# A gated linear attention and a mixture of experts: the blanking DMA and the weight loads are queued elsewhere, and a range check moves to ScalarE

## The chip, the cores and the metric

The kernel runs on one core of a Trainium2 chip. The core has five engines with an instruction queue each: TensorE (PE; its weight loads are shown as PEld), VectorE (DVE), ScalarE (ACT), GpSimd (POOL) and SyncE (SP). An engine takes its instructions strictly in the order of its queue. Loads are issued from SP's queue; the blanking, the scatters and the output go out from POOL's. The metric is the device time of one execution in microseconds, the median of several runs.

## The reference

Two blocks. The first is a recurrence with a complex decay, for 4 batches, 8 heads, 768 steps and head size 48; the second sends each of the 3072 resulting rows of 384 numbers through one of eight experts (384 to 1024 to 384).

```python
mag = np.sqrt(a_re * a_re + a_im * a_im)
scale = np.minimum(mag, 0.999) / (mag + 1e-06)
a_re_n, a_im_n = (a_re * scale, a_im * scale)
for t in range(S):
    new_re = ar * S_re - ai * S_im
    new_im = ar * S_im + ai * S_re
    kv = np.einsum('bhd,bhe->bhde', k[:, :, t], v[:, :, t])
    S_re, S_im = (new_re + kv, new_im)
    y[:, :, t] = np.einsum('bhd,bhde->bhe', q[:, :, t], S_re)
...
logits = x @ w_gate
expert_idx = np.argmax(logits, axis=1)
...
    h = np.maximum(x_sorted[lo:hi] @ w1[e], 0.0)
    y_sorted[lo:hi] = h @ w2[e]
...
return (gate_w[:, None] * y).astype(np.float32)
```

## The kernel before

**Attention.** The rows are cut into 24 chunks of 128, and two chunks make a unit `u` (0 to 11). The decay of a unit is turned into logarithm and angle by five steps, `decay_steps`, that go back and forth between POOL (products of `ar` and `ai`), DVE and ACT (Ln and Exp, then Arctan in another table). `decay_sums` takes running sums of the logarithm on PE (`csl`) and turns them into two factors `E` and `Ei` on ACT; `decay_total` makes the factor `M` of a whole chunk from `ms`; `angle_sums` and `rotation` make cosine and sine, `CS`. For each chunk `attention` multiplies `q` and `k` by the factors (`product`: `Qe` and `Ke` on POOL, `Q` and `K` on DVE), transposes them (`tp`), forms scores `at`, masks them to `am`, and sums `y`, which ACT copies into `x`. While unit `u` is in its attention, the decay of unit `u + 1` is prepared. The copies `ar`, `ai`, `q`, `k`, `v` of a unit live in two buffers each, and `ai` is overwritten with the angle `th`, so that a load of `ai` waits until the angle sums of two units before are done.

**Routing.** Every four chunks, `route` picks an expert for 512 rows and scatters them into a DRAM buffer `xs` that has 448 places for each expert (`NS` = 3584 rows in all). Unused places must hold a zero row with an index that drops it, so `blank` writes 5.4 MB of `zrow` over `xs` ahead of the first scatter, from POOL's queue.

**Experts.** Each of eight experts reads its rows with `gather`, transposes them (`turn`), and computes in `expert` eight tiles `hps` of 128 hidden units by 448 rows (three matmuls each, in three PSUM buffers), which DVE (even ones) and ACT (odd ones) turn into `ht` in SBUF; then the products `yps` with `w2`, eight matmuls for each of four row tiles. The weights of expert 0 are loaded during the attention (`load_w(0)`, called at `u == 6`), the others two experts ahead.

**Range check.** The attention is only valid while `a_re` is not negative and the squared magnitude is at least 0.37. `range_check` reads both arrays again in 12 pieces of 128 by 768, three pieces for each of four experts, and `verdict` decides whether a slow path has to run; with this data it doesn't.

**What sets the order.** The program is written as above, but a scheduler decides in which order each engine's queue holds the instructions, by data, buffers, its own estimate of times, and by the pairs that `tc.add_manual_dep` ties together without a wait. So a tie moves neighbours too.

Of the kernel before, what the change touches and what calls it, by code (L numbers as in the profile page):

```python
# [35 lines left out]
def kernel(  # L36
# [12 lines left out]
    nc = tc.nc  # L49
# [6 lines left out]
    NT = N // P  # L56
# [25 lines left out]
    def const(shape, name, dt=FP):  # L82
        return cp.tile(shape, dt, name=name)
# [15 lines left out]
        out=last, in_=ones, compare_op=OP.is_ge, fill=0.0, base=1 - P, pattern=[[0, P]], channel_multiplier=1  # L99
# [19 lines left out]
    zrow = const([P, XW], "zrow")  # L119
# [5 lines left out]
    xs = dr.tile([ZR + P, XW], FP, name="xs")  # L125

    def blank():

        nc.gpsimd.dma_start(out=xs[0:NS].rearrange("(i p) c -> p i c", p=P), in_=bc(zrow, 1, NS // P))
        nc.gpsimd.dma_start(out=xs[ZR : ZR + P], in_=zrow)  # L130

    W_T = {}

    def load_w(e):
        a = wp[e % 2].tile([P, KD, F], FP, tag="w1", name="w1t")
        nc.sync.dma_start(out=a, in_=w1[e].rearrange("(i p) f -> p i f", p=P))
        b = wp[e % 2].tile([P, KF, DM], FP, tag="w2", name="w2t")
        T["w"] = nc.sync.dma_start(out=b, in_=w2[e].rearrange("(i p) d -> p i d", p=P))
        W_T[e] = a, b


    xl = ctx.enter_context(tc.tile_pool(name="xl", bufs=2))
    psL = ctx.enter_context(tc.tile_pool(name="psL", bufs=1, space=PSUM))
    att = ExitStack()
    ld = att.enter_context(tc.tile_pool(name="ld", bufs=2))
# [8 lines left out]
    T = {}  # L154

    def act(**kw):

        ins = nc.scalar.activation(**kw)  # L158
        if "act" in T:
            tc.add_manual_dep(ins.ins, T["act"].ins.name, NOSYNC, reason="table order")  # L160
        T["act"] = ins

    def table(name):
        ins = nc.scalar.preload_act_table_set(name)
        if "act" in T:
            tc.add_manual_dep(ins.ins, T["act"].ins.name, NOSYNC, reason="table order")
        T["act"] = ins

    def load(u, names):
        for nm, src in names:  # L170
            t = ld.tile([P, U, H, D], FP, tag=nm, name=nm)
            for c in range(U):
                b, s = divmod(u * U + c, CB)
                nc.sync.dma_start(out=t[:, c], in_=src[b, :, s * P : (s + 1) * P, :].rearrange("h t d -> t h d"))
            T[nm, u] = t.rearrange("p c h d -> p (c h d)")

    def load_a(u):
# [97 lines left out]
    def product(u, c, nm, src, dec):  # L275
        sl = slice(c * DM, (c + 1) * DM)
        e = ch.tile([P, H, D], FP, tag=nm + "e", name=nm + "e")
        nc.gpsimd.tensor_tensor(
            out=e.rearrange("p h d -> p (h d)"), in0=T[src, u][:, sl], in1=T[dec, u][:, sl], op=OP.mult
        )  # L280
        t = ch.tile([P, H, 2, D], FP, tag=nm, name=nm)
        nc.vector.tensor_tensor(out=t, in0=T["CS", u][:, c * H : (c + 1) * H], in1=bc(e, 2, 2), op=OP.mult)  # L282
        return t.rearrange("p h a d -> p h (a d)")
# [140 lines left out]
    for u in range(NU):  # L424
        if u + 1 < NU:
            load_qkv(u + 1)
        if u == 1:
            blank()
        steps = decay_steps(u + 1) if u + 1 < NU else []
        steps = steps[:2] + [lambda: decay_sums(u, 0)] + steps[2:4] + [lambda: decay_sums(u, 1)] + steps[4:]  # L430
        table("natural_log_exp_and_others")
        if u > GR // U and (u - 1) * U % GR == 0:
            route((u - 1) * U - GR, False)
        for f in steps:
            f()
# [92 lines left out]

    CW = 768
    NC = B * H * S * D // (P * CW)  # L530
    good = const([P, NC], "good")
    flat = [a.rearrange("b h s d -> (b h s d)").rearrange("(p n) -> p n", p=P) for a in (a_re, a_im)]

    def range_check(i):
        ar = ck.tile([P, CW], FP, tag="car", name="car")
        ai = ck.tile([P, CW], FP, tag="cai", name="cai")
        for t, a in zip((ar, ai), flat):
            ld = nc.sync.dma_start(out=t, in_=a[:, i * CW : (i + 1) * CW])
            tc.add_manual_dep(ld.ins, T["w"].ins.name, NOSYNC, reason="behind the weights")
        s = ck.tile([P, CW], FP, tag="cs", name="cs")  # L540
        nc.gpsimd.tensor_tensor(out=s, in0=ar, in1=ar, op=OP.mult)
        nc.gpsimd.tensor_tensor(out=ai, in0=ai, in1=ai, op=OP.mult)
        nc.gpsimd.tensor_tensor(out=s, in0=s, in1=ai, op=OP.add)
        nc.vector.scalar_tensor_tensor(out=s, in0=s, scalar=-MAG2_MIN, in1=ar, op0=OP.add, op1=OP.min)
        nc.vector.tensor_reduce(out=good[:, i : i + 1], in_=s, op=OP.min, axis=AX_X)

    def verdict():

        bad = xl.tile([P, NC], FP, tag="bad", name="bad")
        nc.vector.tensor_scalar(out=bad, in0=good, scalar1=0.0, scalar2=None, op0=OP.is_ge)  # L550
        nc.vector.tensor_scalar(out=bad, in0=bad, scalar1=-1.0, scalar2=1.0, op0=OP.mult, op1=OP.add)
        two = xl.tile([P, 2], FP, tag="two", name="two")
        nc.vector.reduce_sum(two[:, 0:1], bad, axis=AX_X)
        nc.vector.reduce_sum(two[:, 1:2], ov, axis=AX_X)
        nc.vector.tensor_tensor(out=two[:, 1:2], in0=two[:, 1:2], in1=two[:, 0:1], op=OP.add)
        bp = psX.tile([1, 2], FP, tag="tp", padded_shape=[1, 512], name="bp")
        mm(bp, ones[:, 0:1], two)
        nc.vector.tensor_copy(out=flag, in_=bp)

    flag = const([1, 2], "flag", I32)  # L560
    rest0 = [P] * ((CAP - FIRST) // P) + [HT]
    own = [P] * (CT - 1) + [HT]
    for e in range(E):
# [154 lines left out]
```

## Time and profile before

| what | value |
|---|---|
| median of 3 runs | 811.48 us (809.31 to 820.83) |
| profiled execution | 809.06 us, its span 807.4 us |
| mean granted TensorE clock | 0.89 |
| busy: PE, PEld | 698.9, 510.5 us |
| busy: DVE, POOL, ACT | 348.6, 278.1, 207.7 us |
| DMA | 79.60 MB, 99 GB/s over the span |

The profile is one execution. The span runs from the first to the last instruction; the execution's own time is 1.7 us longer. The attention fills about the first 465 us (the last copy of `y` starts at 464.9), the experts the rest. Times in a timeline are counted from the start of the span, and the bracket behind a row is the engine's idle time before it with what ended it.

### The profile page before, as it was taken

What the parts mean: (1) busy time and instruction counts of PE and PEld (TensorE: products, weight loads), DVE (VectorE), ACT (ScalarE), POOL (GpSimd) and SP (SyncE); (2) the same over time, 40 slices, a digit from 0 to 9 for tenths busy, and PEclk for the clock granted to TensorE, in tenths of its full rate; (3) what the DMA queues carried; (4) which work ended last, traced back from release to release, by engine and by line L of the source; (5) the groups of instructions that cost most, each with busy time, mean ns of one, the idle gap of its engine ahead of it and who ended that gap; (6) DMA issues with size and microseconds to landing.
All of it is one profiled execution on the core that took longest, in us unless ns stands there. A gap on an engine that the chain in (4) does not pass through costs nothing. (4 is left out here: it accounts for less than half of the span.)

```text
span 807.4 us, 9049 instructions
## 1 busy us (share of the span) xinstructions
PE 698.9 (87%) x3583; PEld 510.5 (63%) x3583; DVE 348.6 (43%) x577; ACT 207.7 (26%) x338; POOL 278.1 (34%) x216
## 2 busy tenths in 40 slices
PE   0057899989799998998989999999998989898994
PEld 0036788868689877887878977554544545454552
DVE  2137466655766767664555331202133342425211
ACT  3225343342526525344333110101010101000000
POOL 4353360643365255253321011000053443526101
PEclk9999879768878968885887889999999999999998
DMA  9952432233144243313010152523272635352000
GB/s 263 290 150 48 81 60 40 50 89 69 36 102 89 40 86 74 78 30 88 2 21 11 50 186 85 192 97 125 97 240 91 219 115 205 132 180 72 27 11 24
DMA packets 148817, 79.60 MB, mean 99 GB/s; under 512 B 127278, under 2 KB 139071, under 8 KB 148768
## 3 DMA queue, kind: packets, MB, share of 16 engines
q1 hardware_dynamic: 144032, 63.75, 29.7%
q0 software_dynamic: 4736, 15.20, 5.2%
q8 instruction: 30, 0.49, 0.2%
q14 instruction: 19, 0.16, 0.1%
HBM read 63.74 MB, written 15.98 MB: 99 GB/s over the span
## 5 line engine op out<-in xcount | busy, mean ns | idle before, releaser
L71 PE MATMUL hps<-xt,w1t 128*128 128x448 f32 (+2 forms) x432 | 154.9, 518 | 11.2 <-DVE ht L506 11.2
L71 PE MATMUL yps<-w2t,ht 128*128 128x384 f32 (+1 forms) x512 | 147.2, 488 | 0.0
L71 PEld LDWEIGHTS hps<-xt,w1t 128*128 128x128 f32 x432 | 83.0, 198 | 75.5 <-issue 58.6
L71 PEld LDWEIGHTS yps<-w2t,ht 128*128 128x128 f32 (+1 forms) x512 | 81.7, 177 | 64.7 <-issue 16.1
L487 POOL DMA_INDIRECT out_dram<-y,xg x32 | 31.1, 971 | 205.7 <-DVE y L515 174.0
L71 PE MATMUL y<-v,am 128*128 128x48 f32 x384 | 75.7, 292 | 0.0
L71 PE MATMUL y<-G,qt 96*128 96x48 f32 x320 | 69.0, 301 | 0.0
L71 PEld LDWEIGHTS y<-v,am 128*128 128x128 f32 x384 | 63.9, 213 | 4.3 <-DVE am L377 1.7
L515 DVE TENSOR_SCALAR y<-yps,xg 128x384 f32<-128x384 f32 x24 | 14.8, 617 | 113.8 <-PE yps L71 113.8
L71 PE MATMUL at<-qt,kt 96*128 96x128 f32 x384 | 59.3, 299 | 3.5 <-DVE am L377 3.2
L71 PE MATMUL csl<-LL,tri 128*128 128x384 f32 x48 | 25.5, 618 | 40.9 <-DVE LL L214 34.2
L71 PEld LDWEIGHTS at<-qt,kt 96*128 96x128 f32 x384 | 54.2, 211 | 9.1 <-issue 4.4
L71 PE MATMUL ms<-ones,LL 128*96 128x1 f32 x384 | 51.5, 267 | 8.0 <-ACT Ei L158 8.0
L71 PEld LDWEIGHTS ms<-ones,LL 128*96 128x96 f32 x384 | 51.5, 234 | 9.7 <-ACT Ei L158 9.1
L504 ACT ACTIVATE ht<-hps 128x448 f32<-128x448 f32 (+2 forms) x36 | 18.1, 503 | 150.5 <-PE hps L71 150.5
L71 PEld LDWEIGHTS y<-G,qt 96*128 96x128 f32 x320 | 56.0, 218 | 0.6 <-issue 0.6
L369 PE MATMUL tp<-ident,Q 128*96 128x128 f32 x192 | 40.4, 333 | 16.2 <-DVE Q L282 16.2
L349 POOL DMA_INDIRECT xs<-x,to x24 | 26.9, 1122 | 77.6 <-DMA xs<-x,to 34.4
L506 DVE TENSOR_SCALAR ht<-hps 128x448 f32<-128x448 f32 (+2 forms) x36 | 20.5, 570 | 74.6 <-PE hps L71 74.5
L258 DVE TENSOR_SCALAR r<-cst 128x384 f32<-128x384 f32 x24 | 13.4, 557 | 82.7 <-PE cst L71 82.7
L369 PE MATMUL tp<-ident,K 128*96 128x128 f32 x192 | 40.0, 328 | 5.3 <-DVE K L282 5.3
L200 POOL TENSOR_TENSOR A<-A,R 128x768 f32<-128x768 f32 x12 | 23.6, 1967 | 55.0 <-ACT R L158 44.4
(117 smaller groups left out, 1035.5 us busy)
## 6 DMA issues: line engine op xcount, KB each, us to landing
w1t<-in_moe_w_dram SPq DMA_DIRECT2D x8, 1536.0 KB, 6.3
w2t<-in_moe_w_dram SPq DMA_DIRECT2D x8, 1536.0 KB, 6.8
xs<-zrow POOLq DMA_DIRECT2D x1, 5404.0 KB, 20.0
ar<-in_a_re_dram SPq DMA_DIRECT2D x24, 192.0 KB, 3.2
ai<-in_a_im_dram SPq DMA_DIRECT2D x24, 192.0 KB, 3.4
q<-in_q_dram SPq DMA_DIRECT2D x24, 192.0 KB, 3.4
k<-in_k_dram SPq DMA_DIRECT2D x24, 192.0 KB, 3.6
v<-in_v_dram SPq DMA_DIRECT2D x24, 192.0 KB, 3.2
```

The source lines that it names most:

```text
L71: return nc.tensor.matmul(o, lhsT=lhsT, rhs=rhs, start=start, stop=stop, skip_group_check=True)
L200: nc.gpsimd.tensor_tensor(out=A, in0=A, in1=R, op=OP.mult)
L258: nc.vector.tensor_scalar(out=r, in0=cs, scalar1=MAGIC, scalar2=MAGIC, op0=OP.add, op1=OP.subtract)
L349: nc.gpsimd.indirect_dma_start(out=xs[:, :], out_offset=bass.IndirectOffsetOnAxis(ap=to[:, i : i + 1], axis=0), in_=x[:, i], in_offset=None,)
L369: nc.tensor.transpose(out=tp[0:DD, j], in_=X[:, hg * 4 + j], identity=ident)
L487: return nc.gpsimd.indirect_dma_start(out=out, out_offset=bass.IndirectOffsetOnAxis(ap=idx, axis=0), in_=y[0:m], in_offset=None, bounds_ch ...
L504: nc.scalar.activation(out=ht[:, f], in_=ps, func=AF.Relu)
L506: nc.vector.tensor_scalar(out=ht[:, f], in0=ps, scalar1=0.0, scalar2=None, op0=OP.max)
L515: nc.vector.tensor_scalar(out=y, in0=ps, scalar1=gate, scalar2=None, op0=OP.mult)
```

## The change

Three edits.

The blanking is called after the attention of chunk 0, and both of its DMAs are tied behind `T["K"]`, POOL's product `Ke` of that chunk. The first weight load of an expert, `w1`, is tied behind `T["ld"]`, the load that was written last when `load_w` is called; the second, `w2`, gets no tie. In the range check ACT makes both squares and finds violations with Relu and the running sum that an activation can write (`accum_out`); POOL keeps only the sum of the squares, and DVE does nothing until the verdict.

```diff
     def blank():
-        nc.gpsimd.dma_start(out=xs[0:NS].rearrange("(i p) c -> p i c", p=P), in_=bc(zrow, 1, NS // P))
-        nc.gpsimd.dma_start(out=xs[ZR : ZR + P], in_=zrow)
+        for o, i in ((xs[0:NS].rearrange("(i p) c -> p i c", p=P), bc(zrow, 1, NS // P)), (xs[ZR : ZR + P], zrow)):
+            queue(nc.gpsimd.dma_start(out=o, in_=i), T["K"])
...
+    def queue(ins, before):
+        tc.add_manual_dep(ins.ins, before.ins.name, NOSYNC, reason="queue order")
+        return ins
...
     def load_w(e):
         a = wp[e % 2].tile([P, KD, F], FP, tag="w1", name="w1t")
-        nc.sync.dma_start(out=a, in_=w1[e].rearrange("(i p) f -> p i f", p=P))
+        ins = nc.sync.dma_start(out=a, in_=w1[e].rearrange("(i p) f -> p i f", p=P))
+        queue(ins, T["ld"])
...
-                nc.sync.dma_start(out=t[:, c], in_=src[b, :, s * P : (s + 1) * P, :].rearrange("h t d -> t h d"))
+                T["ld"] = nc.sync.dma_start(out=t[:, c], in_=src[b, :, s * P : (s + 1) * P, :].rearrange("h t d -> t h d"))
...
-        nc.gpsimd.tensor_tensor(
+        T[nm] = nc.gpsimd.tensor_tensor(
...
-        if u == 1:
-            blank()
...
+        if u == 0:
+            blank()
...
         s = ck.tile([P, CW], FP, tag="cs", name="cs")
-        nc.gpsimd.tensor_tensor(out=s, in0=ar, in1=ar, op=OP.mult)
-        nc.gpsimd.tensor_tensor(out=ai, in0=ai, in1=ai, op=OP.mult)
+        nc.scalar.activation(out=s, in_=ar, func=AF.Square)
+        nc.scalar.activation(out=ai, in_=ai, func=AF.Square)
+        nc.scalar.activation(out=ar, in_=ar, func=AF.Relu, scale=-1.0, accum_out=bad[:, 0, i : i + 1])
         nc.gpsimd.tensor_tensor(out=s, in0=s, in1=ai, op=OP.add)
-        nc.vector.scalar_tensor_tensor(out=s, in0=s, scalar=-MAG2_MIN, in1=ar, op0=OP.add, op1=OP.min)
-        nc.vector.tensor_reduce(out=good[:, i : i + 1], in_=s, op=OP.min, axis=AX_X)
+        nc.scalar.activation(out=s, in_=s, func=AF.Relu, scale=-1.0, bias=mag2, accum_out=bad[:, 1, i : i + 1])
```

Lines of the kernel after are five higher in the attention. What the scheduler makes of it stands in three places.

POOL's queue at the start, before. In the names, `_137`, `_140` and `_160` belong to unit 0, `_153`, `_156` and `_189` to unit 1, `_338` and `_355` to unit 2; `Qe_255` and `Ke_259` are chunk 0.

```order
L129 DMA xs_106<-zrow_102 128x28x386
L200 TENSOR_TENSOR A_160<-A_160,R_162 128x768
L193 TENSOR_TENSOR A_189<-ar_153 128x768
L194 TENSOR_TENSOR R_191<-ai_156 128x768
L130 DMA xs_106<-zrow_102 128x386
L347 COPY x_325<-tidi_100 128x4
L213 TENSOR_TENSOR ai_140<-ai_140,A_160 128x768
L193 TENSOR_TENSOR A_355<-ar_338 128x768
L200 TENSOR_TENSOR A_189<-A_189,R_191 128x768
L278 TENSOR_TENSOR Qe_255<-q_143,E_201 128x384
L278 TENSOR_TENSOR Ke_259<-k_146,Ei_202 128x384
```

Here the blanking (L129) and the products of unit 1's load stand ahead of unit 0's `ai` product (L213), and a product of unit 2's load ahead of unit 1's L200. After, from unit 0's `ai` product on (`_340` and `_343` are unit 2 now, `Qe_422` is chunk 1):

```order
L218 TENSOR_TENSOR ai_140<-ai_140,A_160 128x768
L198 TENSOR_TENSOR A_189<-ar_153 128x768
L199 TENSOR_TENSOR R_191<-ai_156 128x768
L205 TENSOR_TENSOR A_189<-A_189,R_191 128x768
L283 TENSOR_TENSOR Qe_255<-q_143,E_201 128x384
L283 TENSOR_TENSOR Ke_259<-k_146,Ei_202 128x384
L130 DMA xs_106<-zrow_102 128x28x386
L218 TENSOR_TENSOR ai_156<-ai_156,A_189 128x768
L130 DMA xs_106<-zrow_102 128x386
L198 TENSOR_TENSOR A_355<-ar_340 128x768
L199 TENSOR_TENSOR R_357<-ai_343 128x768
L283 TENSOR_TENSOR Qe_422<-q_143,E_201 128x384
```

Unit 0's `ai` product moved ahead of unit 1's loads, unit 1's chain and chunk 0's products ahead of the blanking, and chunk 1's products behind the products of unit 2's loads.

SP's queue, before, from unit 1's last load on (`_338`, `_341`, `_344`, `_347` are unit 2, `ar_604` is unit 3; `w1t` and `w2t` are expert 0's weights).

```order
L174 DMA v_186<-in_v_dram 128x8x48 x2
L136 DMA w1t_1965<-in_moe_w1_dram 128x3x1024
L174 DMA ar_338<-in_a_re_dram 128x8x48 x2
L138 DMA w2t_1967<-in_moe_w2_dram 128x8x384
L174 DMA ar_604<-in_a_re_dram 128x8x48 x2
L174 DMA q_344<-in_q_dram 128x8x48 x2
L174 DMA k_347<-in_k_dram 128x8x48
L174 DMA ai_341<-in_a_im_dram 128x8x48 x2
```

After (`_340`, `_343`, `_346`, `_349` are unit 2, `ar_869` is unit 4):

```order
L179 DMA v_186<-in_v_dram 128x8x48 x2
L179 DMA ar_340<-in_a_re_dram 128x8x48 x2
L179 DMA ar_604<-in_a_re_dram 128x8x48 x2
L145 DMA w2t_1967<-in_moe_w2_dram 128x8x384
L179 DMA ai_343<-in_a_im_dram 128x8x48 x2
L179 DMA q_346<-in_q_dram 128x8x48 x2
L179 DMA k_349<-in_k_dram 128x8x48 x2
L179 DMA ar_869<-in_a_re_dram 128x8x48 x2
```

The load of `w1t` left this place for one behind unit 8's `ai`; `w2t` stayed, ahead of unit 2's `ai`, `q` and `k`.

ACT's queue beside a range check, before: transposed rows `xt`, the four odd hidden tiles, the last row tile's copy.

```order
L74 COPY xt_3960<-tp_3967 128x448
L504 ACTIVATE ht_3982<-hps_3988 128x448
L504 ACTIVATE ht_3982<-hps_3998 128x448
L504 ACTIVATE ht_3982<-hps_4008 128x448
L504 ACTIVATE ht_3982<-hps_4018 128x448
L522 COPY y_4066<-yps_4065 64x384
```

After, from behind the first odd hidden tile to ahead of the third (`car_3932`, `car_3942` and `car_3952` are the three pieces' `ar`, with `cai` and `cs` to match; `ht_3984<-hps_4000` is the second odd tile):

```order
L548 ACTIVATE cs_3936<-car_3932 128x768
L550 ACTIVATE car_3932,bad_3502<-car_3932 128x768
L549 ACTIVATE cai_3933<-cai_3933 128x768
L548 ACTIVATE cs_3946<-car_3942 128x768
L509 ACTIVATE ht_3984<-hps_4000 128x448
L552 ACTIVATE cs_3936,bad_3502<-cs_3936,mag2_3503 128x768
L549 ACTIVATE cai_3943<-cai_3943 128x768
L550 ACTIVATE car_3942,bad_3502<-car_3942 128x768
L548 ACTIVATE cs_3956<-car_3952 128x768
L552 ACTIVATE cs_3946,bad_3502<-cs_3946,mag2_3503 128x768
L550 ACTIVATE car_3952,bad_3502<-car_3952 128x768
L549 ACTIVATE cai_3953<-cai_3953 128x768
```

Eleven of the twelve new ACT instructions stand between the first and the third odd tile; the twelfth, `cs_3956` into `bad_3502`, stands between the third and the fourth.

## Rows read from the trace of the kernel before

**Rows 1.** windows: PE, PEld, DVE, ACT, POOL busy us (instructions), PEclk, DMA share, GB/s
```profile
0.00:20.00 20.00, 0.00 (x0) 0.00 (x0) 4.55 (x11) 6.78 (x7) 8.79 (x18) 1.00 0.95 262
...
120.00:160.00 40.00, 38.22 (x270) 34.25 (x269) 27.72 (x52) 16.09 (x26) 13.13 (x9) 0.84 0.24 47
```

**Rows 2.** timeline of POOL, start: start us, us, engine, line, op, tiles [idle before]
```profile
7.99 1.81 POOL L129 DMA_DIRECT2D xs<-zrow  x1
...
28.94 1.47 POOL L193 TENSOR_TENSOR A<-ar 128x768 f32<-128x768 f32 x1 [15.83 <-DMA ar<-in_a_re_dram]
...
33.21 2.52 POOL L213 TENSOR_TENSOR ai<-ai,A 128x768 f32<-128x768 f32 x1
43.53 1.47 POOL L193 TENSOR_TENSOR A<-ar 128x768 f32<-128x768 f32 x1 [7.80 <-DMA ar<-in_a_re_dram]
```

**Rows 3.** DMA queues and issues from 5 to 34 us: packets, MB; us to landing
```profile
q1 hardware_dynamic: 16405, 3.04, 56.2%
q0 software_dynamic: 1219, 5.55, 52.7%
...
xs<-zrow POOLq DMA_DIRECT2D x1, 5404.0 KB, 20.0
...
ar<-in_a_re_dram SPq DMA_DIRECT2D x2, 192.0 KB, 18.0
```

**Rows 4.** page, part 6: DMA issues of one line over the whole span
```profile
ar<-in_a_re_dram SPq DMA_DIRECT2D x24, 192.0 KB, 3.2
```

**Rows 5.** timeline of ACT, the first three units
```profile
14.13 1.72 ACT L158 ACTIVATE A<-A 128x768 f32<-128x768 f32 x2 [0.15 <-DVE A L201]
...
63.39 0.94 ACT L158 ACTIVATE CS<-fg,mhalfpi 128x768 f32<-128x768 f32 x1 [6.38 <-DVE fg L263]
...
65.81 1.28 ACT L164 ACT_TABLE_LOAD   x1
...
77.94 0.48 ACT L402 COPY x<-y 128x384 f32<-128x384 f32 x1 [3.00 <-PE y L71]
...
129.87 0.94 ACT L158 ACTIVATE CS<-fg,mhalfpi 128x768 f32<-128x768 f32 x1 [7.39 <-DVE fg L263]
...
170.00 0.94 ACT L158 ACTIVATE CS<-fg,mhalfpi 128x768 f32<-128x768 f32 x1 [2.21 <-DVE fg L263]
```

**Rows 6.** timeline of PE, the first two units' total-decay matmuls
```profile
50.21 5.28 PE L71 MATMUL ms<-ones,LL 128*96 128x1 f32 x32 [7.99 <-ACT Ei L158]
...
82.03 4.00 PE L71 MATMUL ms<-ones,LL 128*96 128x1 f32 x32
```

**Rows 7.** timeline of PE, experts 1 to 7
```profile
549.01 2.22 PE L478 MATMUL tp<-ident,xg 128*128 128x128 f32 x12
551.16 18.31 PE L71 MATMUL hps<-xt,w1t 128*128 128x448 f32 x48
569.31 18.37 PE L71 MATMUL yps<-w2t,ht 128*128 128x384 f32 x64
587.61 2.22 PE L478 MATMUL tp<-ident,xg 128*128 128x128 f32 x12
...
608.56 4.22 PE L71 MATMUL hps<-xt,w1t 128*128 128x448 f32 x6 [2.75 <-DVE ht L506]
...
757.64 0.19 PE L71 MATMUL bp<-two,ones 128*1 128x2 f32 x2
```

**Rows 8.** windows, PE's columns and granted clock right behind a stall
```profile
608.60:612.60 4.00, 4.00 (x6) 1.95 (x7) 2.15 (x3) 0.00 (x0) 2.50 (x2) 0.57 0.00 0
```

**Rows 9.** timeline of all engines, the first expert that runs beside a range check
```profile
595.52 1.46 POOL L541 TENSOR_TENSOR cs<-car 128x768 f32<-128x768 f32 x1 [3.51 <-DMA car<-in_a_re_dram]
...
603.60 0.54 ACT L504 ACTIVATE ht<-hps 128x448 f32<-128x448 f32 x1 [3.97 <-PE hps L71]
...
605.69 1.47 POOL L542 TENSOR_TENSOR cai<-cai 128x768 f32<-128x768 f32 x1
605.77 2.21 DVE L544 SCALAR_TENSOR_TENSOR cs<-cs,car 128x768 f32<-128x768 f32 x1 [2.25 <-POOL cs L543]
```

More of the change, by code (lines that the diff above doesn't have):

```diff
@@ L127, in blank @@
     def blank():
-        nc.gpsimd.dma_start(out=xs[0:NS].rearrange("(i p) c -> p i c", p=P), in_=bc(zrow, 1, NS // P))
-        nc.gpsimd.dma_start(out=xs[ZR : ZR + P], in_=zrow)
-    W_T = {}
+        for o, i in ((xs[0:NS].rearrange("(i p) c -> p i c", p=P), bc(zrow, 1, NS // P)), (xs[ZR : ZR + P], zrow)):
+            queue(nc.gpsimd.dma_start(out=o, in_=i), T["K"])
+    T, W_T = {}, {}
+    def queue(ins, before):
+        tc.add_manual_dep(ins.ins, before.ins.name, NOSYNC, reason="queue order")
+        return ins
     def load_w(e):
         a = wp[e % 2].tile([P, KD, F], FP, tag="w1", name="w1t")
-        nc.sync.dma_start(out=a, in_=w1[e].rearrange("(i p) f -> p i f", p=P))
+        ins = nc.sync.dma_start(out=a, in_=w1[e].rearrange("(i p) f -> p i f", p=P))
+        queue(ins, T["ld"])
         b = wp[e % 2].tile([P, KF, DM], FP, tag="w2", name="w2t")
@@ L152 @@
     psD = att.enter_context(tc.tile_pool(name="psD", bufs=1, space=PSUM))
-    T = {}
     def act(**kw):
@@ L159, in act @@
         if "act" in T:
-            tc.add_manual_dep(ins.ins, T["act"].ins.name, NOSYNC, reason="table order")
+            queue(ins, T["act"])
         T["act"] = ins
@@ L165, in table @@
         if "act" in T:
-            tc.add_manual_dep(ins.ins, T["act"].ins.name, NOSYNC, reason="table order")
+            queue(ins, T["act"])
         T["act"] = ins
@@ L530 @@
     NC = B * H * S * D // (P * CW)
-    good = const([P, NC], "good")
+    bad = const([P, 2, NC], "bad")
+    mag2 = const([P, 1], "mag2")
+    nc.vector.memset(mag2, MAG2_MIN)
     flat = [a.rearrange("b h s d -> (b h s d)").rearrange("(p n) -> p n", p=P) for a in (a_re, a_im)]
@@ L537, in range_check @@
         for t, a in zip((ar, ai), flat):
-            ld = nc.sync.dma_start(out=t, in_=a[:, i * CW : (i + 1) * CW])
-            tc.add_manual_dep(ld.ins, T["w"].ins.name, NOSYNC, reason="behind the weights")
+            queue(nc.sync.dma_start(out=t, in_=a[:, i * CW : (i + 1) * CW]), T["w"])
         s = ck.tile([P, CW], FP, tag="cs", name="cs")
-        nc.gpsimd.tensor_tensor(out=s, in0=ar, in1=ar, op=OP.mult)
-        nc.gpsimd.tensor_tensor(out=ai, in0=ai, in1=ai, op=OP.mult)
+        nc.scalar.activation(out=s, in_=ar, func=AF.Square)
+        nc.scalar.activation(out=ai, in_=ai, func=AF.Square)
+        nc.scalar.activation(out=ar, in_=ar, func=AF.Relu, scale=-1.0, accum_out=bad[:, 0, i : i + 1])
         nc.gpsimd.tensor_tensor(out=s, in0=s, in1=ai, op=OP.add)
-        nc.vector.scalar_tensor_tensor(out=s, in0=s, scalar=-MAG2_MIN, in1=ar, op0=OP.add, op1=OP.min)
-        nc.vector.tensor_reduce(out=good[:, i : i + 1], in_=s, op=OP.min, axis=AX_X)
+        nc.scalar.activation(out=s, in_=s, func=AF.Relu, scale=-1.0, bias=mag2, accum_out=bad[:, 1, i : i + 1])
     def verdict():
-        bad = xl.tile([P, NC], FP, tag="bad", name="bad")
-        nc.vector.tensor_scalar(out=bad, in0=good, scalar1=0.0, scalar2=None, op0=OP.is_ge)
-        nc.vector.tensor_scalar(out=bad, in0=bad, scalar1=-1.0, scalar2=1.0, op0=OP.mult, op1=OP.add)
+        nc.vector.tensor_scalar(out=bad, in0=bad, scalar1=0.0, scalar2=None, op0=OP.is_gt)
         two = xl.tile([P, 2], FP, tag="two", name="two")
-        nc.vector.reduce_sum(two[:, 0:1], bad, axis=AX_X)
+        nc.vector.reduce_sum(two[:, 0:1], bad.rearrange("p a i -> p (a i)"), axis=AX_X)
         nc.vector.reduce_sum(two[:, 1:2], ov, axis=AX_X)
@@ L682, in others @@
                     expert([P], turn([P], xg), wa, wb, xg)
-    with tc.If(nc.values_load(flag[0:1, 1:2], min_val=0, max_val=P * (NC + NT)) > 0):
-        with tc.If(nc.values_load(flag[0:1, 0:1], min_val=0, max_val=P * NC) > 0):
+    with tc.If(nc.values_load(flag[0:1, 1:2], min_val=0, max_val=P * (2 * NC + NT)) > 0):
+        with tc.If(nc.values_load(flag[0:1, 0:1], min_val=0, max_val=P * 2 * NC) > 0):
             slow_attention()
```

## The prediction

> **What bounds the kernel now.** I read the busy time by stretch first, then the waits at the head, then the experts. For the first 20 us PE does nothing while the DMA engines are 95% busy; in the attention PE is busy 38.2 of 40 us, at a granted clock of 0.84 [rows 1]. So whatever starts the attention sooner moves all of it forward, and inside it there is little idle time to win. Among the experts PE has no gap except beside the range check [rows 7].
>
> The head: the blanking is issued at 7.99 us and lands 20.0 us later [rows 2, 3]. POOL then waits 15.83 us for unit 1's `ar` and another 7.80 us for unit 2's [rows 2]. Behind the first wait stands unit 0's `ai` product, which had nothing to do with that load: ACT finished its input at 14.13 + 1.72 = 15.85 us, and it started at 33.21 [rows 2, 5].
>
> The experts: an expert without a range check takes 587.61 - 549.01 = 38.6 us from transposes to transposes; the four with one take 757.64 - 587.61 = 170.0 us, 42.5 each [rows 7]. The excess is 170.0 - 4 x 38.6 = 15.6 us. It is a PE wait for DVE's `ht` of 2.75 us in the expert shown (the other three are alike), and a granted clock of 0.57 behind it [rows 7, 8], which in two of the four experts adds almost 2 us more. DVE is late because in its queue the check's combine stands ahead of that `ht`, and waited 2.25 us for POOL's sum [rows 9].
>
> **The blanking moved.** It removes POOL's first wait and the jam under it. Replay: unit 0's `ai` product starts at 15.9 instead of 33.2 us. Unit 1's two products follow; a product takes 1.47 to 2.52 us [rows 2], so with 1.8 for the first and 1.47 each for the other two they end at 20.6 (before: two of 1.47 from 28.94 on, 32). Their loads are then there: without the jam a load lands in 3.2 us instead of 18.0 [rows 3, 4], and nothing larger is queued ahead. From there to the first `ms` on PE took 50.21 - 32 = 18.2 us [rows 6], of which 7.80 was the wait for unit 2's `ar` and 1.47 the product it blocked; in the new order neither stands ahead. 18.2 - 9.3 = 8.9, so `ms` starts at 29.5, **20.7 us sooner**. The first rotation `CS` follows 13.2 later, as before, at 42.7, and the first copy of `x` 14.55 after that, at 57 [rows 5, 6].
>
> Not all of that stays. The blanking now starts behind `Ke` of chunk 0, which ends at about 28.5 (20.6, a DVE step of about 1, two activations of 0.86, a POOL product of 1.8, two products of half the width at 1 to 1.8). Its 20.0 us reach to 48.5. Expert 0's `w2t`, 1.5 MB, was not tied and is in flight with it; at 3.04 + 5.55 MB in 29 us, which is what the two queues of [rows 3] moved, it adds 5 us. Unit 2's `ai` is behind it with two loads of 0.2 MB and their latency: about 56. POOL's products of chunk 1 stand behind that load, and ACT's steps for unit 2 now stand behind the first copy of `x`, with Arctan and a table load between. Before, they ran ahead of it: table load at 65.81, second `ms` at 82.03, 16.2 us [rows 5, 6], with waits for PE in them; the bare chain (table 1.28, six activations of 0.86, four half ones of 0.5, a POOL product of 1.8, a DVE step of about 1) is 11. After: `x` at 57, Arctan and copies to 59, then 11 to 16: second `ms` at 70 to 75 instead of 82.03. I take the middle, 72.5, because the chain has PE's transposes between its steps here too but fewer of chunk 1's: the head keeps **10 us** (7 to 12; if the load is hidden altogether up to 20.7, if it is later than 57 one us less for each us).
>
> **The weights moved.** `w1t` leaves the head; that is the 7.80 us wait, counted already. It goes behind unit 8's `ai`, where 1.5 MB hold up the loads behind it by about 5 us. They are `v` of unit 7 first, not read before that unit's attention. The DMA engines are 24% busy in such a stretch [rows 1], so I take nothing; the bounds are 0 and 5 us.
>
> **The range check on ACT.** It removes 24 POOL squares and 24 DVE instructions and adds 48 activations of 128 by 768, at 0.86 us each [rows 5]; the running sum has no row, so an activation with it costs between 0.86 and, doubled, 1.72. I take 0.9, since it writes one number for each partition beside the same elements. Three pieces are 12 x 0.9 = 10.8 us of ACT in an expert that has 18 us of `hps`. No `ht` may be late: eight tiles take 569.31 - 551.16 = 18.15 us, 2.27 each [rows 7], so the odd ones are ready at 594.5, 599.1, 603.60 and 608.1 on the scale of [rows 9]. With three PSUM buffers, tile 3 has to be out when tile 6 starts, at 603.6. Tiles 5 and 7 are read by the sixth and eighth matmul of the first row tile of `yps`, which starts at 607.9 and takes about 18.37 / 3.5 = 5.2: at 611.2 and 612.5.
>
> ACT in the order shown: `car` arrives at 595.52 [rows 9]; four activations to 599.1; tile 3 from 599.1 to 599.7, due by 603.6. POOL's sum, started at 598.2, is out by 600.1 at the latest; the next steps, to the third piece's Relu, are six of 0.9 and end near 605.5, or a little after. The third `cai`, which in both programs waits for POOL's first sum, was being squared at 605.69 [rows 9]. So: square 606.6, tile 5 done 607.2 (due 611.2), POOL's last sum 609, Relu 610, tile 7 done 610.6 (due 612.5). Everything is in time, with 1.8 us to spare. The 2.75 us waits go, and the low clock with them: **15 us** of the 15.6, bounds 0 and 15.6 for this order with its margin. DVE's and POOL's lighter load is free, because PE waits for neither elsewhere in this stage.
>
> **The sum.** 809.06 (the profiled execution, 1.7 us beyond its span, and 2.4 below the median of 811.48) - 10 - 15 = 784.
>
> **Rivals.** *The jam only moves.* [Rows 3] show why a load lands so late beside the blanking: 1219 packets of it hold 5.55 MB, 16405 of the loads 3.04 MB, and both get through at about the same time. If unit 3's `ar` and, behind it, unit 2's `ai` each take the 18.0 us of unit 1's `ar`, `ai` lands at 28.5 + 36 = 64.5, some 8 us later than I put it, and the head keeps 2: 809 - 2 - 15 = 792. For it speaks that `w2t` is still in the way; against it that the blanking is over by about 54 whatever is beside it, and unit 3's `ar` may be through before it starts. [...]
>
> *ACT becomes what DVE was.* Tile 7 has 1.8 us to spare behind a chain ACT, POOL, ACT. If the running sum costs half an activation more, 6 x 0.43 = 2.6 us are added, and PE waits 0.8 us and gets the low clock, some 2.7 us an expert; if the third piece lands 3 us late, as much as today. Then 809 - 10 = 799, or 795 for half.
>
> *The scheduler's new order is worse.* PE's queue differs through about the first six units and is alike from there. Units are not alike before: units 1 and 2 took (129.87 - 63.39) / 2 = 33.2 us each, unit 3, with a routing step, 170.00 - 129.87 = 40.1 [rows 5]. If the reordered six all ran like the worst one, 6 x 6.9 = 41 us would be lost and the time would be 825; it is slower than before from 25 / 6 = 4.2 us a unit on. For it: PE waits in its order, and the clock falls behind waits. Against it: the same instructions with the same dependences, and unit 3 may as well improve.
>
> *More stays.* Chunk 1's products are not late and unit 3 runs like its neighbours: 809 - 16 - 15 - 7 = 771.
>
> **How the numbers follow.** Forecast 0.50 (776 to 792); the jam moves 0.18 (792); ACT late 0.12 (795 to 799); worse order 0.09 (811 to 825); more stays 0.11 (769 to 775). The range 769 to 801 leaves out the worse order and a little at the tails. A measurement here tells about 2%, 16 us, from no change: faster than 795 is 0.50 + 0.11 and two thirds of the jam case, 0.73; slower than 828 is beyond the worst rival's price, 0.06; the rest 0.21.
>
> **What would show it.** Right: the first `ms` near 29 us and no POOL wait over 5 us ahead of it; the blanking issued near 28; the second `ms` at 70 to 75; four experts at 38.6 to 39 us, no PE wait for `ht`, clock 1.00 throughout. Wrong: unit 2's `ai` landing after 60; a PE wait for ACT's `ht` at the start of `yps`; units 1 to 6 longer than 34 us on average.

## The result, and the profile of the changed kernel

| | before | after |
|---|---|---|
| runs beside each other, median (lowest to highest), us | 810.7 (809.31 to 820.83, 4 runs) | 788.33 (785.32 to 790.33, 4 runs) |
| ratio, 95% interval | | 0.9695 [0.9608, 0.9782] |
| profiled execution / its span, us | 809.06 / 807.4 | 786.72 / 784.7 |
| mean granted clock of TensorE | 0.890 | 0.869 |

The kernel became 3% faster: 22.3 us between the profiled executions, 22.4 between the medians. Executions over 1.5% above the fastest of the same kernel are left out of a ratio, here and below, but not out of the medians. The mean clock is lower although the program is shorter, and that line turns out to matter.

**The head.** The timeline of the changed kernel, rows of several engines in order of time (they answer to [rows 2, 5, 6]; its lines in the attention stand 5 further down than in the kernel before):

```profile
15.84 1.80 POOL L218 TENSOR_TENSOR ai<-ai,A 128x768 f32<-128x768 f32 x1 [2.89 <-ACT A L163]
...
28.11 1.82 POOL L130 DMA_DIRECT2D xs<-zrow  x1
28.38 0.69 SPq L145 DMA_DIRECT2D w2t<-in_moe_w_dram  x1
29.01 5.28 PE L71 MATMUL ms<-ones,LL 128*96 128x1 f32 x32 [3.12 <-ACT Ei L163]
39.16 1.90 SPq L179 DMA_DIRECT2D ai<-in_a_im_dram  x2
42.19 0.94 ACT L163 ACTIVATE CS<-fg,mhalfpi 128x768 f32<-128x768 f32 x1 [6.39 <-DVE fg L268]
54.17 1.47 POOL L199 TENSOR_TENSOR R<-ai 128x768 f32<-128x768 f32 x1 [19.77 <-DMA ai<-in_a_im_dram]
54.58 0.48 ACT L407 COPY x<-y 128x384 f32<-128x384 f32 x1 [6.17 <-PE y L71]
67.72 2.84 PE L71 MATMUL ms<-ones,LL 128*96 128x1 f32 x32
82.26 0.94 ACT L163 ACTIVATE CS<-fg,mhalfpi 128x768 f32<-128x768 f32 x1
```

Unit 0's `ai` product starts at 15.84 us instead of 33.21 and the first `ms` at 29.01 instead of 50.21: 21.2 us sooner. POOL then waits 19.77 us for unit 2's `ai`. The second `ms` is 14.3 us sooner than before (67.72 to 82.03), the second rotation 14.7 (82.26 to 96.95). The DMA issues of the changed kernel between 24 and 60 us, with the median time from issue to landing, name what that wait was for:

```profile
xs<-zrow POOLq DMA_DIRECT2D x1, 5404.0 KB, 24.6
w2t<-in_moe_w_dram SPq DMA_DIRECT2D x1, 1536.0 KB, 12.5
...
ai<-in_a_im_dram SPq DMA_DIRECT2D x2, 192.0 KB, 14.5
```

The jam of [rows 3] is still there; another load stands in it.

**The experts with the range check.** Timeline of the changed kernel, TensorE, ScalarE and GpSimd in one of the four (answering to [rows 7, 9]), and below it the window over all four:

```profile
582.88 18.31 PE L71 MATMUL hps<-xt,w1t 128*128 128x448 f32 x48
599.12 0.52 ACT L509 ACTIVATE ht<-hps 128x448 f32<-128x448 f32 x1
599.29 1.81 POOL L551 TENSOR_TENSOR cs<-cs,cai 128x768 f32<-128x768 f32 x1 [2.70 <-ACT cai L549]
601.03 18.37 PE L71 MATMUL yps<-w2t,ht 128*128 128x384 f32 x64
601.13 0.93 ACT L552 ACTIVATE cs<-cs,mag 128x768 f32<-128x768 f32 x1 [1.49 <-POOL cs L551]
602.06 0.52 ACT L509 ACTIVATE ht<-hps 128x448 f32<-128x448 f32 x1
619.33 2.21 PE L483 MATMUL tp<-ident,xg 128*128 128x128 f32 x12
```

```profile
580.73:735.12 154.39, 154.25 (x499) 82.23 (x497) 26.02 (x47) 52.38 (x96) 37.24 (x28) 1.00 0.48 167
```

No PE row has a wait in brackets. PE is busy 154.25 of 154.39 us at a clock of 1.00: 38.6 us an expert, where the four took 170.0: 15.6 us less. The last `ht` is done at 602.58; the eighth matmul of `yps` reads it at about 601.03 + 7/8 of 5.25 = 605.6, so 3 us were to spare.

**What does not add up.** 14.7 us at the second rotation and 15.6 in the four experts are 30.3; the program gained 22.3. From the second rotation to expert 1's `tp` the changed kernel took 503.55 - 82.26 = 421.3 us, the kernel before 510.41 - 96.95 = 413.5: 7.8 us went there. The windows from the second to the last copy of `x`, first of before, then of after, show how (PE busy, and the granted clock third from the end):

```profile
95.46:464.92 369.46, 338.81 (x2294) 300.82 (x2294) 225.91 (x384) 150.75 (x242) 141.60 (x103) 0.80 0.26 57
```

```profile
80.77:454.80 374.03, 346.32 (x2294) 308.43 (x2294) 226.26 (x384) 150.93 (x243) 144.34 (x103) 0.77 0.27 61
```

These are the same 2294 matmul records. PE was idle less (27.7 us instead of 30.7) and busy longer, at a lower clock. From the last copy of `x` to expert 1 it is the same again: 45.49 us at 0.92 before, 48.75 at 0.84 after. The experiments had to say whether the change did that.

### The profile page after: what moved, and what is told of

Read it like the earlier page. It is cut to its first block, busy times and chain, and to the rows that moved or that the text cites. A ratio compares the mean times of both kernels' runs of the same rounds, so it can differ in the third digit from the quotient of the medians.

```text
span 784.7 us, 9067 instructions
## 1 busy us (share of the span) xinstructions
PE 709.1 (90%) x3583; PEld 522.5 (67%) x3583; DVE 320.0 (41%) x553; ACT 247.7 (32%) x410; POOL 242.1 (31%) x192
## 5 line engine op out<-in xcount | busy, mean ns | idle before, releaser
L71 PEld LDWEIGHTS yps<-w2t,ht 128*128 128x128 f32 (+1 forms) x512 | 81.4, 177 | 64.1 <-issue 15.6
L71 PE MATMUL at<-qt,kt 96*128 96x128 f32 x384 | 61.8, 308 | 2.1 <-DVE am L382 1.8
L71 PEld LDWEIGHTS at<-qt,kt 96*128 96x128 f32 x384 | 56.1, 218 | 8.3 <-issue 2.6
L374 PE MATMUL tp<-ident,Q 128*96 128x128 f32 x192 | 42.4, 350 | 19.2 <-DVE Q L287 19.2
L71 PE MATMUL ms<-ones,LL 128*96 128x1 f32 x384 | 49.3, 262 | 3.9 <-ACT Ei L163 3.9
L71 PEld LDWEIGHTS ms<-ones,LL 128*96 128x96 f32 x384 | 49.0, 225 | 5.6 <-ACT Ei L163 5.2
L74 ACT COPY qt<-tp 96x512 f32<-96x512 f32 x48 | 27.9, 581 | 63.6 <-PE tp L374 63.4
L374 PEld LDWEIGHTS tp<-ident,Q 128*96 128x96 f32 x192 | 29.2, 169 | 26.5 <-DVE Q L287 24.3
```

What stands on the lines that cost most here:

```text
L71: return nc.tensor.matmul(o, lhsT=lhsT, rhs=rhs, start=start, stop=stop, skip_group_check=True)
L74: (nc.scalar.copy if i % 2 else nc.vector.tensor_copy)(out=o, in_=in_)
L374: nc.tensor.transpose(out=tp[0:DD, j], in_=X[:, hg * 4 + j], identity=ident)
```

## The experiments

Every ratio below is against the kernel before on the same chip. Its median there was 819.3 us beside `head_only`, `check_only`, `w2_tied` and `busy_head`; 824.8 beside `before_again`, `weights_free`, `wide_ms` and `act_more1`; 821.9 beside `wide_kept`, `blank_later`, `before_wide` and `w2_wide`.

### Each part alone

`head_only` has the moved blanking and weights, with the range check of before; `check_only` is the kernel before with the new range check.

```
 head_only:   def range_check(i): ... as before (DVE and POOL)
 check_only:  blank() at u == 1, no queue(ins, T["ld"]), as before
```

> The changed kernel with the range check of before (on VectorE and GpSimd). Theory, two separate gains: the stretch up to the second pair of rotation Sines is as in the changed kernel (second rotation at 82 us, before 96.95), 6.9 us of it are left at expert 1, the last four experts take 170 us again: 802 us profiled. Rival, the check alone made the gain: the first gain is all lost by the end of the attention, 807 to 809 us. Rival, the two help each other: the four experts take less than 168 us.

> The kernel before with the range check of the change (ScalarE's running sums) and nothing else. Theory, two separate gains: the stretch up to expert 1 is as before to within 1 us (its tp at 510 us), the four experts with the check take 154.4 us instead of 170.0: 793.5 us profiled. Rival, the check helps only because the attention was re-timed: over 797 us. If the attention's clock differs from run to run by itself, the start of expert 1 moves by several us though nothing ahead of it was changed.

Measured: `head_only` 804.05 us, ratio 0.9821 [0.9746, 0.9897]; `check_only` 806.40, 0.9851 [0.9783, 0.9919]. A row of the timeline of `head_only`, TensorE, and the window over its four experts:

```profile
603.64 2.52 PE L71 MATMUL hps<-xt,w1t 128*128 128x448 f32 x6 [2.71 <-DVE ht L511]
```

```profile
582.73:752.35 169.62, 158.71 (x498) 83.37 (x497) 57.60 (x72) 12.75 (x24) 77.31 (x52) 0.98 0.45 152
```

And of `check_only`, the window alone:

```profile
602.14:756.53 154.39, 154.24 (x498) 82.36 (x496) 26.02 (x47) 52.39 (x96) 37.17 (x28) 1.00 0.48 167
```

The check is worth the same 15.2 to 15.6 us with either head, and it is the wait for DVE's `ht`, 2.71 us in the row shown, that goes. In `head_only` the second rotation is at 81.26 us, as in the changed kernel. The gains are separate, and as far as these runs tell both reach the end: the ratios are worth about 15 and 12 us, each uncertain by about 6, and their product, 0.9675, is near the 0.9695 of the changed kernel. My 793.5 us for `check_only` missed all the same. Its instructions stand in the order of before up to expert 1, and it reached that at 524.95 us instead of 510.41: order alone does not set the length of the attention.

### What jams the head

`w2_tied` takes `w2t` out of the jam, `weights_free` puts `w1t` into it, `blank_later` takes the blanking out of it.

```diff
 w2_tied:
         T["w"] = nc.sync.dma_start(out=b, in_=w2[e]...)
+        queue(T["w"], T["ld"])
 weights_free:
-        queue(ins, T["ld"])
 blank_later:
-        if u == 0:
+        if u == 1:
             blank()
```

> The changed kernel with w2 of expert 0 tied behind the attention's loads as w1 is: 1.5 MB fewer go between 28 and 41 us. Theory, what holds the second unit is the jam of the blanking, w2 and unit 2's loads: the second ai of unit 2 lands near 49 us instead of 53.7, the first x copy comes at 50 instead of 54.6, the second ms at 63 instead of 66.7, and of these 4 us about half is left at the end: 785 us. Rival, the blanking's writes alone hold the loads: the first x copy stays at 54 and the time at 786 to 787. Rival, two weight loads in the middle of the attention now cost it: over 788.

> The changed kernel without the tie of w1: expert 0's w1t and w2t go out where the scheduler puts them, w1t ahead of unit 2's ai and w2t behind it. Theory, the jam counts in bytes: unit 2's second ai lands 1 to 6 us later than in the changed kernel (55 to 60), the first x copy at 55 to 60, the second ms at 67 to 72, the whole 787 to 792. Rival, the tie of w1 does nothing: 786 to 788. Rival, w1t in the middle of the attention costs what it saves in the head: under 786.

> The changed kernel with the blanking called one unit later, so tied behind K of chunk 2 instead of chunk 0. Theory, the blanking only jams what is loaded beside it and can be put where nothing is late: unit 2's second ai lands before 48 us instead of at 53.7, the first x copy at 49 to 51, the second ms at 62 to 64, and the second x copy of each later unit is not later for it: 3 to 5 us sooner in the attention, 782 to 786 in all. Rival, the jam only moves to unit 3's loads: the gain at the first x copy is gone by the fifth, 786 to 790.

Measured: `w2_tied` 787.91 us, 0.9616 [0.9543, 0.9689]; `weights_free` 789.64, 0.9520 [0.9399, 0.9641]; `blank_later` 779.24, 0.9512 [0.9439, 0.9584]. POOL's row behind unit 2's `ai`, of `w2_tied`, of `weights_free` and of `blank_later`:

```profile
50.04 1.47 POOL L200 TENSOR_TENSOR R<-ai 128x768 f32<-128x768 f32 x1 [15.32 <-DMA ai<-in_a_im_dram]
```

```profile
55.93 1.47 POOL L198 TENSOR_TENSOR R<-ai 128x768 f32<-128x768 f32 x1 [21.22 <-DMA ai<-in_a_im_dram]
```

```profile
43.24 1.47 POOL L199 TENSOR_TENSOR R<-ai 128x768 f32<-128x768 f32 x1 [8.33 <-DMA ai<-in_a_im_dram]
```

The load is issued at 39.2 to 39.5 us in all four and lands after 3.0 us with no large transfer beside it, 9.9 beside the blanking, 14.5 beside the blanking and `w2t`, 15.8 beside the blanking and `w1t`. So 1.5 MB more cost 4.6 to 5.9 us; I had estimated 5. The weights cost it by making the blanking longer: in the changed kernel `w2t` has landed at 40.9 us, the blanking lands at 52.7 (`w2_tied` 48.6, `weights_free` 54.4), and the load within 1.1 us of it in all three. `w2t` itself was issued 0.3 us behind the blanking and landed 11.8 us ahead of it; how the two queues share the DMA engines, these runs do not show.

What I expected of the next steps was wrong, but for `weights_free`. The first copy of `x` did not follow the load: it came at 53.79, 55.04 and 57.34 us, beside 54.58 in the changed kernel. It waits for chunk 0's own matmuls, and in `blank_later` PE and ACT did unit 2's steps ahead of it. The second `ms` follows the load: 66.40, 69.87 and 57.14 us, beside 67.72. Of the 10.6 us in `blank_later`, 4.2 are left at the second copy of `x`, 4.6 at the fifth, where the rival had nothing left, and 5.1 at expert 1 (498.43 to 503.55, on different chips). The other two differ from the changed kernel by less than these runs can tell, so neither `w2t` in the jam nor `w1t` in the middle of the attention shows in the time of these few runs.

### ScalarE's room in the experts

```diff
+        nc.scalar.activation(out=s, in_=ar, func=AF.Square)
         nc.scalar.activation(out=s, in_=ar, func=AF.Square)
...
```

> The changed kernel with one more Square of 128 by 768 into the same tile on ScalarE for each of the 12 pieces, and TensorE's order held as it is by ties. The scheduler then lists 14 activations of the check between the second and the fourth tile's ht on ScalarE, where there were 4 between them. Theory, ScalarE's list has little room: 14 of about 0.87 us end 5 us after the seventh hps, which needs that tile's PSUM buffer, so TensorE waits some 5 us in each of the four experts, its clock falls behind the wait, and the four take 174 to 187 us instead of 154.4. Rival, ScalarE is not what these experts hang on: 154 to 157 us.

Measured: 793.45 us in its one run, the four experts 742.01 - 583.69 = 158.3 us, and a clock of 1.00 over them. Timeline of `act_more1`, one expert, PE, ACT and DVE:

```profile
585.84 16.05 PE L71 MATMUL hps<-xt,w1t 128*128 128x448 f32 x42
601.93 0.62 DVE L513 TENSOR_SCALAR ht<-hps 128x448 f32<-128x448 f32 x1 [3.88 <-PE hps L71]
602.61 2.52 PE L71 MATMUL hps<-xt,w1t 128*128 128x448 f32 x6 [0.72 <-DVE ht L513]
603.78 0.52 ACT L511 ACTIVATE ht<-hps 128x448 f32<-128x448 f32 x1
604.97 18.37 PE L71 MATMUL yps<-w2t,ht 128*128 128x384 f32 x64
605.90 0.96 ACT L511 ACTIVATE ht<-hps 128x448 f32<-128x448 f32 x2
```

Neither theory held: 1.0 us an expert, not 5 and not 0. ACT reads its second tile, the fourth of the eight, only at 603.78, yet PE had run seven tiles by 601.9. So the seventh tile was not bound to the buffer of the fourth, three before it. Unread by then were the fourth, the sixth and the seventh, one in each buffer, and PE waited for the eighth until DVE had read the seventh. The margin on ScalarE was wider than the strict turn of buffers in my working.

### The clock of the attention

`before_again` is the kernel before, unchanged. `busy_head` gives TensorE work in the head that nothing reads or waits for:

```diff
+        if u == 0:
+            y = psY.tile([P, DM], FP, tag="y", padded_shape=[P, 512], name="y")
+            for i in range(72):
+                mm(y[:, 0:P], ident, ones)
```

> The kernel before once more, unchanged, for a second profile of it. Theory, the 7.8 us that the changed kernel seems to lose between the second rotation and expert 1 are a difference between two executions in the clock that the attention was granted, and the first profile of the kernel before caught a good one: expert 1's tp starts at 514 to 523 us here instead of 510.41, the stretch from the second to the thirteenth x copy has a clock under 0.82, and the four experts with the check take 170 us again. Rival, the new order of the attention costs the 7.8 us: 510 to 511 us, 0.82.

> The kernel before with 72 matmuls of 128x128 in a PSUM tile that is not read, run by TensorE in the first 40 us, where it has nothing to do; nothing waits for them. Theory, the attention is held by the granted clock and TensorE's rest in the head is paid back by a higher clock later: the stretch from the second to the thirteenth x copy takes 187 to 193 us instead of 185.3 at a clock under 0.82, and the whole 812 to 816 us. Rival, the clock in the attention does not depend on what TensorE did in the head: 185.3 us, 809 us in all.

Measured: `before_again` 828.63 us in its one run. Its second rotation is at 97.04 us (before: 96.95) and expert 1's `tp` at 530.02 (510.41), past the 523 that I allowed: 19.5 us between two executions of one program, 16.1 of them between the second and the last copy of `x` (`check_only`, with the same order there, lies between: 524.95). Window from the second to the last copy of `x`, of `before_again`:

```profile
95.54:481.11 385.57, 355.63 (x2294) 316.65 (x2294) 223.39 (x384) 150.53 (x243) 144.70 (x103) 0.75 0.25 55
```

The same matmuls kept PE busy 16.8 us longer at 0.75 than at 0.80, and PE was idle 29.9 us instead of 30.7. So the missing 7.8 us are well inside what the kernel before does to itself. Its first profile was a lucky one: 809.06 was the lowest of all its runs. The chip of that profile is not on record, but one chip is enough for such a difference: on the one of `head_only`, two runs of the kernel before took 810.64 us at a mean clock of 0.886 and 821.59 at 0.872.

`busy_head` took 825.17 us, ratio 1.0074 [1.0021, 1.0127]. The windows of the head, of `busy_head`:

```profile
24.00:48.00 24.00, 3.26 (x4) 1.00 (x4) 2.39 (x3) 4.68 (x6) 9.08 (x7) 0.50 0.97 253
48.00:72.00 24.00, 15.01 (x57) 10.56 (x58) 12.53 (x13) 9.48 (x13) 10.79 (x8) 0.50 0.38 83
```

and of the kernel before:

```profile
24.00:48.00 24.00, 3.26 (x4) 1.00 (x4) 3.60 (x4) 5.52 (x7) 10.93 (x9) 1.00 1.04 268
48.00:72.00 24.00, 16.68 (x78) 12.19 (x78) 12.82 (x15) 10.16 (x14) 8.94 (x6) 1.00 0.34 66
```

The clock column differs: behind the 19 us of extra matmuls (1.54 to 20.55 us) it shows 48 us at 0.50, where before shows 1.00. The matmuls do not differ. The same four records take 3.26 us from 24 to 48 us in both, and a pair of `csl` takes 1.62 us in either head, against 0.88 later (and 1.63 at 169.15 us, in a part of the attention at 0.50). Timeline of PE, two rows of before, then one of `busy_head`:

```profile
34.21 1.62 PE L71 MATMUL csl<-LL,tri 128*128 128x384 f32 x2 [34.21 <-DVE LL L214]
74.40 0.88 PE L71 MATMUL csl<-LL,tri 128*128 128x384 f32 x2
```

```profile
35.58 1.62 PE L71 MATMUL csl<-LL,tri 128*128 128x384 f32 x2 [15.04 <-DVE LL L214]
```

So the 1.00 in the head of the kernel before stands beside matmuls at the slow pace, and this run does not show that what PE did earlier slowed anything later. Whether the extra work costs the attention is not settled: its stretch was 376.9 us at 0.78, between the two profiles of before, and 0.4 to 1.8 of the 6 us of the ratio are lost in the head already (first rotation at 65.23 us, before 63.39 and 64.83).

### Can the attention's clock be moved?

The 192 `ms` matmuls (384 records in the trace, the number in the expectation) have one column and a weight load each. `wide_ms` gives them 32 columns, of which one is used; the scheduler prices them higher and lays another order. `wide_kept` has the 32 columns with TensorE's order chained, instruction by instruction, to that of the changed kernel. `before_wide` and `w2_wide` are the kernel before and `w2_tied` with the edit of `wide_ms`.

```diff
-        ms = psM.tile([P, U, H], FP, tag="mm", padded_shape=[P, 32, 16], name="ms")
+        ms = psM.tile([P, U * H, 32], FP, tag="mm", name="ms")
...
-                mm(ms[0:DD, c, h : h + 1], L[:, c * H + h], ones[:, 0:1])
+                mm(ms[0:DD, c * H + h], L[:, c * H + h], ones[:, 0:32])
...
 wide_kept, besides:
+    line = [made[f"I-{i}"] for i in ORDER if f"I-{i}" in made]
+    for a, b in zip(line, line[1:]):
+        queue(b, a)
```

> The changed kernel with the column sums ms taken against 32 columns of ones in place of one, of which the first is used; the matmul count stays at 384 and each is bounded by its weight load, 0.27 us. The scheduler's order on TensorE changes with it. Theory, the attention is as long as the granted clock lets it be, and the ms with their one column are where it falls: the clock from the second to the thirteenth x copy rises over 0.80 from 0.78 and the whole falls under 780. Rival, the width is nothing to the clock: 786 to 790. Rival, 31 more columns in 384 matmuls cost TensorE time: over 790.

> The changed kernel with ms against 32 columns of ones, as in the run before, but with TensorE's whole order chained to that of the changed kernel, so that only the width differs there. Theory, width: the clock of the attention rises as it did with the scheduler's own order (0.82 and 0.81), and the whole falls under 770 us. Rival, it was the new order that made it (fewer or earlier ms in a row): the clock stays at 0.78 and the whole at 785 to 790. Between, 770 to 785: some of each.

> The kernel before with ms against 32 columns of ones, in the order that the scheduler then makes. Theory, the attention's clock is set by what TensorE does there and not by the change studied: it falls by 20 to 35 us here as it did in the changed kernel, and the spread of its runs, 20 us, narrows. Rival, only the changed kernel's attention is open to it: within 8 us of the kernel before.

> The changed kernel with both weights tied behind the attention's loads and ms against 32 columns, the two edits that did not cost. Theory, they add: 742 to 757 us, under both kernels by over 30. Rival, w1 and w2 together in the middle of the attention cost what the wide ms gives there: over 765.

Measured: `wide_ms` 756.84 us (742.25 to 758.51, without a ratio); `wide_kept` 785.36, 0.9570 [0.9506, 0.9635]; `before_wide` 783.75, 0.9539 [0.9475, 0.9603]; `w2_wide` 750.28, **0.9137 [0.9081, 0.9194]**. Windows from the second to the last copy of `x`, of `wide_kept`, then of `w2_wide`:

```profile
83.67:457.55 373.88, 344.20 (x2294) 306.82 (x2294) 219.94 (x384) 151.51 (x242) 138.91 (x103) 0.77 0.27 60
```

```profile
75.97:423.48 347.51, 320.76 (x2294) 289.71 (x2293) 227.01 (x383) 150.07 (x243) 146.55 (x104) 0.83 0.31 70
```

My theory of the width fell: with TensorE's order kept, 32 columns change nothing (373.9 us at 0.77, the changed kernel 374.0 at 0.77). It is the order, or the width only together with it; no run has the new order with one column. The same stretch in the profiles (`blank_later` and `before_wide` cut it six records shorter):

| kernel | stretch, us | PE busy, us | not busy, us | clock |
|---|---|---|---|---|
| before, first and second profile | 369.5, 385.6 | 338.8, 355.6 | 30.7, 29.9 | 0.80, 0.75 |
| `check_only`, `busy_head` | 381.8, 376.9 | 352.0, 347.0 | 29.9, 30.0 | 0.76, 0.78 |
| after | 374.0 | 346.3 | 27.7 | 0.77 |
| `head_only`, `act_more1` | 376.9, 377.3 | 347.1, 350.2 | 29.8, 27.1 | 0.77, 0.76 |
| `w2_tied`, `blank_later` | 381.8, 372.9 | 355.4, 345.9 | 26.4, 27.1 | 0.75, 0.77 |
| `wide_kept` | 373.9 | 344.2 | 29.7 | 0.77 |
| `w2_wide`, `before_wide` | 347.5, 340.5 | 320.8, 316.2 | 26.8, 24.3 | 0.83, 0.84 |

PE is not busy for 24 to 31 us in every row; the stretch goes with the clock. `w2_wide` against `w2_tied` is 34 us shorter in it, with the idle time unchanged (26.8 and 26.4 us). The sum of PE's pauses hardly differs (24.3 to 30.7 us) while the stretch differs by over 30 us, so that sum does not explain it; whether their places do was not shown, nor which of the moved instructions matters.

The traces do show where the clock falls. In windows of half a microsecond, the parts of this stretch at 0.50 add up to 150 and 190 us in the two profiles of before, to 194 in `w2_tied` and to 115 in `w2_wide`. In the profiles of before such a part begins during a unit's `ms` block, or within 1 us of it, at nine and at ten of the ten blocks. What differs is how long it lasts. Behind the block at 151 us the first profile is low for 24 us, the second for 41; windows of the two:

```profile
151.50:175.50 24.00, 21.42 (x90) 17.65 (x90) 9.68 (x19) 6.69 (x9) 10.63 (x8) 0.50 0.42 98
```

```profile
151.50:192.50 41.00, 38.36 (x175) 33.67 (x174) 17.94 (x29) 14.31 (x23) 17.68 (x13) 0.50 0.30 68
```

That `ms` makes the clock fall is not shown by this: in `wide_kept`, with 32 columns, seven of the ten blocks have it too, and the parts at 0.50 add up to as much as in the changed kernel (168 and 170 us).

`w2_wide` is over 8% faster than the kernel before, and in its time below the changed kernel by 38 us (on different chips).

## Why the prediction came out as it did, step by step

The time was right to half a percent (784 forecast, 786.72 profiled, 788.33 median), and in the head and in the experts the mechanisms were those named. That it was so close is partly luck. Three sizes were off and partly covered each other: 809.06 - 14.7 - 15.6 + 7.8 = 786.6, and without the 7.8 us, which the prediction did not have, it would have been 779.

- **The blanking's first wait.** Right: `ms` at 29.5 forecast, 29.01 found; the blanking issued at 28.5 and 28.11; no POOL wait over 5 us ahead of it.
- **What the jam takes back.** Unit 2's `ai` at 56 forecast, 53.7 found (39.16 + 14.5), and the bytes of `w2t` at their price. The step behind it was mis-sized: I let unit 2's decay steps begin only behind the first copy of `x`, at 57. That copy was at 54.58, and the second `ms` came 13.1 us later, inside the chain's 11 to 16, where I had begun the chain 2 us behind the copy. It was the load that the steps followed, as `blank_later` showed. At 67.72 the `ms` is below my 70 to 75, and the head kept 14.7 us at the rotation, not 10.
- **The weights.** Taken as nothing between 0 and 5; putting `w1t` back (`weights_free`) makes no difference that can be measured.
- **The range check.** 15 forecast of 15.6; all of it came. I took 0.9 us for an activation: a Square took 0.83 us, a Relu with its running sum 0.83 or, with a bias from a tile, 0.93, and a read of the sum 0.19 behind it. The rival that ACT becomes what DVE was is out: 3 us to spare at the last tile instead of 1.8, and with 12 activations more (three an expert) PE waited 0.72 us an expert. That the seventh tile needs the buffer of the fourth, as I had it, does not hold in the trace of `act_more1`.
- **The attention between.** This is where the sum failed: "whatever starts the attention sooner moves all of it forward". I carried the head's gain to the end unchanged, against an attention that was one execution's. The stretch to expert 1 took 413.5 us in that execution, 433.0 in the second profile of before, 429.3 in `check_only` and 421.3 in the changed kernel. The 7.8 us are not a cost of the change that these runs could show: beside the experiments the kernel before had medians of 819 to 825 us, and against those the variants with both parts of the change and no wide `ms` read 0.951 to 0.962.
- **The other rivals.** The jam only moving is refuted by the 14.7 us. The scheduler's order being worse had as its sign units 1 to 6 over 34 us on average, and that did show: 34.7 from the first rotation to unit 6's ((250.28 - 42.19) / 6; before 33.9). It was the jam in unit 1, 40.1 us to before's 33.6 and 27.9 in `blank_later`; units 2 to 6 took 33.6 on average, before 34.0. So the sign was badly chosen. That "the clock falls behind waits" is more than the traces show: behind the four waits of 2.6 to 3.1 us in the experts of before it was 0.57 twice and 1.00 twice. And I weighed order by waits alone, where `w2_wide`, in another order and with the wide `ms`, took 34 us less with the idle time unchanged.

## What to carry to other kernels

A gain in the head and a gain in a late stage can each be read off the trace, but a sum made against one execution inherits the granted clock of the stretch between (0.80 and 0.75 in the two profiles of before, 369.5 and 385.6 us); look at the lowest and highest run, and profile the kernel before twice, before believing a difference of 1%. A large transfer moved out of the way of one load stands beside another (here unit 2's `ai`, which landed after 14.5 us instead of 3.0): put it where the next loads have the most time, and count its bytes at the measured rate (here 4.6 to 5.9 us for 1.5 MB). And where PE is busy over 90% of the time (320.8 of 347.5 us in `w2_wide`), look at its clock by stretch: `w2_wide`, which differs from `w2_tied` in the width of `ms` and the order that came with it, took 38 us less (on different chips), more than the 22 us of the change. Check the clock against the time of one known matmul, too; in the head the two did not agree (1.62 us for a pair of `csl` at a clock shown as 1.00, 0.88 later).

## What the runs showed of the hardware that was not expected

- One program, in two executions (`before`, `before_again`): 2294 matmul records with PE busy 338.8 us at a clock of 0.80, or 355.6 at 0.75.
- In the first 72 us of the kernel before the granted clock is shown as 1.00, yet a pair of `csl` took 1.62 us at 34 us, as at 0.50 in `busy_head`, and 0.88 at 74 us.
- In the attention nine or ten of the ten `ms` blocks had the clock fall beside them in the two profiles of before, and behind one and the same block, at 151 us, it stayed at 0.50 for 24 or for 41 us.
- A PE wait of 0.72 us an expert in `act_more1` left the clock at 1.00 over all four. Of the four waits of 2.6 to 3.1 us in the kernel before, two were followed by 4 us at 0.57 ([rows 8] and at 693.83 us), two by 4 us at 1.00 (at 651.88 and 736.98).
- A 192 KB load landed in 3.0, 9.9, 14.5 and 15.8 us (`blank_later`, `w2_tied`, the changed kernel, `weights_free`) with nothing, 5.4 MB, and 5.4 + 1.5 MB (twice) beside it or just ahead of it, and in the last three within 1.1 us of the 5.4 MB.
- The running sum of a ScalarE activation shows in the changed kernel as a second instruction of 0.19 us, not as a longer first one (0.83 us with it, 0.83 for a Square without).
